# Attention and squared-ReLU layers on one core: softmax sums inverted in pairs, a copy ranked with the other evacuations, and late tiles marked urgent when their pass ends

## The chip, the cores and the metric

The kernel runs on one core of a Trainium2 chip. A core has five engines with instruction streams of their own: TensorE (PE in the profile; its weight loads are PEld), VectorE (DVE), ScalarE (ACT), GpSimd (POOL) and SyncE (SP), which here issues all transfers. The metric is the device time of one execution in microseconds (us); the lower the better.

## What is computed

Two transformer layers over 2048 rows of width 448, with shared weights. Each layer normalizes the rows, does full multi-head attention with 16 heads of 28 columns, adds the result to the rows, normalizes again, and adds a dense layer with a squared ReLU:

```python
x = x + _A_ref(_layernorm(x, axis=-1), A_wqkv, A_wo)
x = x + _B_ref(_layernorm(x, axis=-1), B_w1, B_b1, B_w2, B_b2)
x = x + _A_ref(_layernorm(x, axis=-1), A_wqkv, A_wo)
x = x + _B_ref(_layernorm(x, axis=-1), B_w1, B_b1, B_w2, B_b2)
```

with, inside `_A_ref` and `_B_ref`,

```python
scores = jnp.einsum("bhqd,bhkd->bhqk", q, k) * scale
p = _softmax(scores, axis=-1)
o = jnp.einsum("bhqk,bhkd->bhqd", p, v)
...
r = jnp.where(h > zero, h, zero)
h = r * r
out = jnp.einsum("bsf,fd->bsd", h, w2) + b2
```

The exponentials of the softmax are the largest single piece of work: 2 layers x 16 heads x 2048 x 2048 of them.

## The kernel before

**Tiles and passes.** The 2048 rows are 16 row tiles of 128. Queries go in blocks of two row tiles, 256 rows (`blocks`); the last two blocks of the second layer have one tile each. The 16 heads form four groups of four (`g` from 0 to 3), whose four heads lie in the four quarters of 32 partitions. A pass is a layer, a block of queries, a group of heads and a range of key tiles. A unit is one head with enough key tiles for 512 columns of scores, so that there are 2048 units. Scores have keys on the partitions and queries in the columns.

**Exponentials on two engines.** Three units make up a tile of scores `sc` of 128 x 1536 in PSUM (`s_stream`). ScalarE takes the exponential of it in one instruction and writes `pt` (`e_stream`). From some tiles one unit is set apart for VectorE, which computes its exponential with a polynomial: `a_unit` reads the scores into `v_i` or a free part of `K_sb`, and `a_rest` does five more steps and writes `pd` or another free buffer. ScalarE then takes only the two others, 128 x 1024. Whether a unit is set apart is decided in `apart`, among other things by how full VectorE has been in the last 12 us of the plan.

**Weighted values and sums.** `p_stream` multiplies the exponentials with the values `V_sb` and adds up a pass in a PSUM bank `oT`. The values carry a column of ones behind each head's 28, so that partition 28 of each quarter of `oT` holds the sums of the exponentials. When a pass is done, the bank is evacuated to `oT_sb` (lines L988, L990).

**Division by the sums.** `norm_stream` inverts the sums of one group and multiplies. For most blocks the sums are first spread over all partitions by a transfer (`spread`, L1026, `dn<-oT_sb`), inverted there by a short reciprocal on VectorE (L1032), stored to DRAM (L1038, `scr<-dn`), and read back to all partitions of their head (L1045, `rec<-scr`); then VectorE multiplies `oT_sb` by `rec` into `oTn` (L1049). That is three transfers, one reciprocal and one multiply for each group. The last block of each layer instead uses a matmul with `sel` and a long reciprocal (L1011, L1017).

**The rest of a block.** Once a block's four groups are done, `chain` does the output projection (`wo`), adds to the rows (L1060), normalizes, does the two dense matmuls with `relu` and `square` (L1104, L1108), and in the first layer normalizes again and projects the second layer's queries, keys and values (`qkv`). `layernorm` turns the normalized rows `xn` on TensorE (L478), and an evacuation copies the turned rows from PSUM to `xnT` (L490).

**What sets the order.** All of it is one program whose order is fixed when it is built. A `Planner` keeps a clock for each engine and a list of streams with priorities, lower numbers first. It picks again and again the instruction that can start soonest by estimated durations and latencies, and the priority decides between equals. Buffers are counted by `Res`. Scores have priority 0, exponentials 1, `p_stream` 2, evacuations of matmuls `EV` = 3.5, blocks' chains 4 and up, and VectorE's steps on a unit set apart 6 (`V_PRIO`), then 3.6 (`V_LATE`) when they have waited 5 us of the plan, then 1.8 (`V_LAST`) when ScalarE is `V_AGE` = 5 tiles past the unit's. When TensorE's load in the plan is low, `s_stream` repeats the score matmuls of a tile, and `heat` inserts matmuls that nothing reads (L1158). A repeated `x18` instead of `x6` in the timeline shows such a tile. So a change of a priority or a buffer moves many instructions of all engines.

Of the kernel before, what the change touches and what calls it, by code (L numbers as in the profile page):

```python
# [11 lines left out]
DT = mybir.dt  # L12
AF = mybir.ActivationFunctionType
ALU = mybir.AluOpType
P = 128
# [39 lines left out]
V_PRIO = 6.0  # L55
V_LATE = 3.6
V_LAST = 1.8
V_AGE = 5
OWN3 = 0
FIRST = 90  # L60
V_FIRST = 9.2
# [7 lines left out]
BUSY = 0.95  # L69
SPAN = 12.0  # L70
NPT = 11
NOS = 4
AEND = 8
HOT = 0.9
MORE = 3
# [140 lines left out]
def kernel(  # L216
# [221 lines left out]
    def layernorm(t0, nt, deps_of, early=False, mv=None, place=None):  # L438


        if mv is None:
            mv = moments()
            for j in range(nt):
                yield stats(mv, t0, j, deps_of(j))
        ln = {}
        single = early and t0 == 0 and TILES
        rss = []
        for a, b in [(0, 1), (1, 2)] if single else [(0, nt)]:
            def rsqrt(e, a=a, b=b):
                rstd = sp.tile([P, 4], DT.float32, name="rstd")  # L450
                for j in range(a, b):
                    ln[j] = rstd[:, j:j + 1]
                ve = sp.tile([P, 4], DT.float32, name="ve")
                nc.gpsimd.tensor_tensor(out=ve[:, a:b], in0=mv[0][:, a:b, 1], in1=eps_t[:, a:b], op=ALU.add)  # L454
                nc.gpsimd.tensor_tensor(out=rstd[:, a:b], in0=ve[:, a:b], in1=mhalf[:, a:b], op=ALU.pow)
            rs = Op("POOL", 0.95, rsqrt, deps=[mv[1][b - 1]], sets=[("rs", t0 + a)] if early else ())
            rss += [rs] * (b - a)
            pl.spawn(EV, iter([rs]))
        box = {}

        def take(e):
# [6 lines left out]
        evs = []  # L468

        def turn(p0, own, xs):  # L470
            box = {}

            def tr(e, xs=xs):
                tp = bank(t, "tp").bitcast(DT.bfloat16).rearrange("p (c q) -> p c q", c=NDC)
                box["t"] = tp
                for k, (xn, _) in enumerate(xs):
                    for dc in range(NDC):
                        nc.tensor.transpose(out=tp[:, dc, k * P:(k + 1) * P],  # L478
                                            in_=xn[:, dc * P:(dc + 1) * P], identity=ident[:, :])
            t = Op("PE", 0.07 * NDC * len(xs), tr, deps=[x[1] for x in xs],  # L480
                   acq=pools_now(early) if early else spare(1))
            yield t

            def ev(e, p0=p0, w=len(xs) * P):
                tp = box["t"]
                dst = xnT[:, :, p0 * P:p0 * P + w]
                if e == "ACT":
                    nc.scalar.copy(out=dst, in_=tp[:, :, 0:w])
                else:
                    nc.vector.tensor_copy(out=dst, in_=tp[:, :, 0:w])  # L490
            o = Op("DVE", 0.12 + 0.3 * len(xs), ev, deps=[t], rel=t, sets=[("xT", t0 + p0)] if early else ())
            ends.append(o)
            evs.extend([o, Op("DVE", 0.0, None, deps=[t], rel=own)])

        wide = 1 if single else 2
        for p0 in range(0, nt, wide):
            js = range(p0, min(p0 + wide, nt))
            own = Op("DVE", 0.0, None, acq=R_xn)
            yield own
            xs = []  # L500
            for j in js:
                xn = xns[2 * (own.turn % 2) + j % 2]

                def norm(e, j=j, xn=xn):
                    nc.vector.tensor_scalar(out=xn[:, 0:D], in0=x_sb[:, t0 + j, :],  # L505
                                            scalar1=mv[0][:, j, 0:1], scalar2=ln[j],
                                            op0=ALU.subtract, op1=ALU.mult)
# [12 lines left out]

    def mm_tile(subs, evac, ev_dur, deps, any_engine=False, sets=(), early=False, post=(), acq=None):
# [343 lines left out]
    def a_unit(gi, x, src, unit, l):  # L865
# [14 lines left out]
                apart_from(gi, t)  # L880
        c = Op("DVE", 0.69, take, deps=[("s", gi)], acq=sets_of(unit), rel=x)
        yield c
        pl.spawn(lambda now: V_LAST if e_now[1] - gi >= V_AGE else V_LATE if now > c.end + V_WAIT else V_PRIO if gi > FIRST else V_FIRST, a_rest(gi, c, box, unit, (b0, b1, b2, b3)))

    def a_rest(gi, c, box, unit, bs):
        b0, b1, b2, b3 = bs
# [24 lines left out]
        yield o  # L911

    norm_done = {}
    oTn_of = {}

    def p_stream():


        for pi, (l, qb, g, kbs, first, last) in enumerate(passes):
# [58 lines left out]
                yield o  # L978
            res = {}
            def ev(e, box=box, first=first, last=last, g=g, res=res, n=n, l=l, qb=qb):  # L980
                src = box["t"][:, 0:n]
# [9 lines left out]
            oe = Op("DVE", 0.15 + n / 930, ev, deps=[o], rel=box["o"], acq=R_os if last else None)  # L991
            yield oe
            if last:
                pl.spawn(3, norm_stream(l, qb, g, res, oe))

    def norm_stream(l, qb, g, res, oe):


        t0, nt = blocks[l][qb]
        n = nt * P  # L1000
        box = {}
        tail = qb == len(blocks[l]) - 1
# [5 lines left out]
        if tail:  # L1008
            def den(e):
                box["t"] = bank(d, "den")  # L1010
                nc.tensor.matmul(box["t"][:, 0:n], lhsT=sel[:, :], rhs=res["t"][:, 0:n], start=True, stop=True)  # L1011
            d = Op("PE", 0.1 + n * 4 / 2400, den, deps=[oe], acq=pools_now())
            yield d

            def rcp(e):
                box["r"] = rp.tile([P, QR], DT.float32, name="rec")
                nc.vector.reciprocal(out=box["r"][:, 0:n], in_=box["t"][:, 0:n])  # L1017
            r = Op("DVE", n * 0.0066, rcp, deps=[d], rel=d, acq=R_rec)
            own = r
            yield r  # L1020
        else:
            w = n // DHP

            def spread(e):
                box["d"] = sp.tile([P, QR // DHP], DT.float32, name="dn")
                nc.sync.dma_start(out=box["d"][:, 0:w],  # L1026
                                  in_=res["t"][DH::DHP, 0:n])
            d1 = Op("DMA", 0.5, spread, deps=[oe], lat=1.0)
            yield d1

            def rcp(e):
                nc.vector.reciprocal(out=box["d"][:, 0:w], in_=box["d"][:, 0:w])  # L1032
            r1 = Op("DVE", 0.25, rcp, deps=[d1])
            yield r1

            def away(e):
                box["s"] = dp.tile([P, w], DT.float32, name=f"scr{w}")
                nc.sync.dma_start(out=box["s"][:, :], in_=box["d"][:, 0:w])  # L1038
            d2 = Op("DMA", 0.4, away, deps=[r1], lat=-0.5)
            yield d2  # L1040

            def back(e):
                box["r"] = rp.tile([P, QR], DT.float32, name="rec")
                src = box["s"][:, :].rearrange("(h a) j -> h (a j)", h=G)
                nc.sync.dma_start(out=box["r"][:, 0:n], in_=src.unsqueeze(1).to_broadcast([G, DHP, n]))  # L1045
            r = own = Op("DMA", 0.5, back, deps=[d2], acq=R_rec, lat=2.7)
            yield r
        def mul(e):
            nc.vector.tensor_tensor(out=oTn_of[l, qb][0][:, g, 0:n], in0=res["t"][:, 0:n],  # L1049
                                    in1=box["r"][:, 0:n], op=ALU.mult)  # L1050
        m = Op("DVE", 0.13 + n / 930, mul, deps=[r, oTn_of[l, qb][1]], rel=oe)
        yield m
        yield Op("DVE", 0.0, None, deps=[m], rel=own)
        norm_done.setdefault((l, qb), []).append(m)
        if len(norm_done[l, qb]) == G:
            pl.spawn(LASTP if (l, qb) == (1, len(blocks[1]) - 1) else NLP + 0.1 * (qb - len(blocks[1])) if l == 1 and qb >= len(blocks[1]) - NL else 4 + 0.1 * qb, chain(l, qb))

    def add_to_x(tb, lo=0, hi=D):
        def f(e, t):
# [147 lines left out]
```

The softmax here doesn't subtract the row's maximum and nothing guards it: scores larger than these inputs give would overflow.

## Time and profile before

| | before |
|---|---|
| time, median of 3 runs | 903.86 us (903.23 to 904.43) |
| span of the profiled execution | 901.8 us |
| busy: TensorE, VectorE, ScalarE | 833.8, 798.2, 874.6 us |
| exponentials on ScalarE | 556 of 128x1536, 127 of 128x1024 |
| transfers `dn<-oT_sb`, `scr<-dn`, `rec<-scr` | 60 each |
| bytes moved by transfers | 18.44 MB |

How to read it: the busy time of an engine is the time in which it executes something, and two instructions that overlap are counted once. A mean duration is that of one instruction by itself, so that a count times a mean can exceed the busy time. An engine that is busy all the time need not be the one that sets the end; the tables by stage and the lists of waits tell that. A wait is put down to the instruction whose end released it.

### The profile page before, as it was taken

The page shows a single profiled execution, that of the slowest core. Times are in us where ns is not written, and L with a number is a line of the kernel's source. Part 1 is how long each engine was busy: PE and PEld are TensorE (multiplying, and loading weights), DVE is VectorE, ACT ScalarE, POOL GpSimd, SP SyncE. Part 2 cuts the span into 40 slices and gives each one's busy share as a digit, 9 for nine tenths or more (in the row PEclk, how much of TensorE's full clock was granted, in tenths as well). Part 3 has the DMA queues.
Part 4 walks back from the last instruction along what each step waited for, and adds up shares of the span by engine and source line. Part 5 has one row for each costly group of instructions (what it writes and reads, how often), then busy time and mean ns, then how long its engine had stood idle before and what let it go on. Part 6 is the DMA issues. An engine that isn't in the chain of part 4 may idle for free.

```text
span 901.8 us, 29143 instructions
## 1 busy us (share of the span) xinstructions
PE 833.8 (92%) x12828; PEld 459.2 (51%) x12828; DVE 798.2 (89%) x1628; ACT 874.6 (97%) x702; POOL 41.8 (5%) x100
## 2 busy tenths in 40 slices
PE   8999999999999989989999999888989999999898
PEld 4555544454545445445455455444454544546566
DVE  7999899899999899987889999989999998998664
ACT  6999999999999999999999999999999999999992
POOL 4100000000000010000000000000000000000000
PEclk9999999999999999989999999999999999999999
DMA  7200100000000000000000000011000000000100
GB/s 224 75 2 3 27 27 8 15 14 9 14 14 9 14 15 8 14 8 8 2 1 3 2 2 2 6 40 34 19 14 25 14 24 14 20 19 14 29 6 22
DMA packets 32987, 18.44 MB, mean 20 GB/s; under 512 B 17498, under 2 KB 32411, under 8 KB 32860
## 3 DMA queue, kind: packets, MB, share of 16 engines
q1 hardware_dynamic: 32860, 16.58, 6.4%
q8 instruction: 100, 1.64, 0.8%
q14 instruction: 27, 0.22, 0.1%
HBM read 14.26 MB, written 2.07 MB: 18 GB/s over the span
## 4 chain that ended last, share of the span: by engine, by line
ACT 72%; issue 13%; PE 9%; DVE 5%; DMA 1%; SPq 0%; ACTq 0%; DVEq 0%
ACT pt L819 72%; PE mt L539 4%; PE sc L795 2%; PE oT L966 1%; DVE st L432 1%; PE sc L539 1%; DMA V_sb<-in_A_wqkv_dram 1%; DVE K_sb L894 1%; DVE v_h L894 0%; DVE xn L505 0%; DVE x_sb L1060 0%; PE mt L1158 0%; DVE mv L433 0%; DVE v_i L877 0%; DVE K_sb L877 0%
## 5 line engine op out<-in xcount | busy, mean ns | idle before, releaser
L819 ACT ACTIVATE pt<-sc 128x1536 bf16<-128x1536 f32 (+1 forms) x683 | 864.6, 1575 | 4.1 <-PE sc L795 3.9
L795 PE MATMUL sc<-Q_sb,K_sb 32*128 32x256 bf16 (+1 forms) x5840 | 324.5, 266 | 55.4 <-ACT pt L819 48.3
L795 PEld LDWEIGHTS <-K_sb 32*128 32x128 bf16 x5840 | 156.6, 92 | 234.2 <-issue 204.2
L966 PE MATMUL oT<-pt,V_sb 128*32 128x256 bf16 (+1 forms) x4094 | 151.4, 268 | 1.9 <-DVE V_sb L589 1.2
L539 PE MATMUL mt<-xnT,w 128*128 128x256 bf16 (+1 forms) x888 | 117.8, 271 | 0.8
L966 PEld LDWEIGHTS <-V_sb 128*32 128x32 bf16 x4352 | 92.6, 96 | 47.2 <-issue 44.0
L894 DVE SCALAR_TENSOR_TENSOR K_sb<-K_sb 128x512 f32<-128x512 uint16 x165 | 112.8, 684 | 1.5 <-PE mt L539 0.9
L894 DVE SCALAR_TENSOR_TENSOR v_h<-v_h,v_i 128x512 f32<-128x512 f32 x142 | 96.9, 682 | 0.5
L539 PEld LDWEIGHTS <-w 128*128 128x128 bf16 x952 | 78.8, 98 | 35.4 <-issue 26.7
L1104 DVE TENSOR_SCALAR r<-mt 128x512 bf16<-128x512 f32 x105 | 71.8, 684 | 11.5 <-PE mt L539 10.8
L539 PE MATMUL mt<-w,V_sb 128*128 128x448 bf16 (+1 forms) x288 | 69.9, 352 | 0.0
L877 DVE TENSOR_SCALAR v_i<-sc 128x512 int32<-128x512 f32 x71 | 48.6, 685 | 9.9 <-PE sc L795 9.3
L1060 DVE TENSOR_TENSOR x_sb<-x_sb,mt 128x448 bf16<-128x448 bf16 (+1 forms) x64 | 39.0, 609 | 11.6 <-PE mt L539 11.3
L894 DVE SCALAR_TENSOR_TENSOR v_h<-v_i 128x512 f32<-128x512 uint16 x71 | 48.6, 685 | 0.5
L454 POOL TENSOR_TENSOR ve<-mv,eps_t 128x2 f32<-128x2 f32 (+1 forms) x34 | 9.0, 264 | 842.7 <-DVE mv L433 782.5
L1158 PE MATMUL mt<-xn,ident 128*128 128x448 bf16 x134 | 45.5, 359 | 1.0 <-DVE oT_sb L990 0.3
L877 DVE TENSOR_SCALAR K_sb<-sc 128x512 int32<-128x512 f32 x55 | 37.6, 684 | 5.6 <-PE sc L795 5.4
L432 DVE BATCH_NORM_STATS2 st<-x_sb 128x6 f32<-128x448 bf16 x64 | 39.6, 618 | 1.1 <-DMA x_sb<-in_A_x_dram 0.7
L539 PEld LDWEIGHTS <-V_sb 128*128 128x128 bf16 x302 | 24.9, 98 | 24.6 <-issue 10.5
L988 DVE COPY oT_sb<-oT 128x256 f32<-128x256 f32 (+1 forms) x48 | 19.0, 396 | 17.0 <-PE oT L966 16.9
L1108 DVE TENSOR_TENSOR V_sb<-r 128x512 bf16<-128x512 bf16 (+1 forms) x73 | 30.0, 414 | 2.5 <-ACT r L1102 1.9
L539 PE MATMUL mt<-wo,oTn 128*128 128x448 bf16 x128 | 31.6, 355 | 0.1
(101 smaller groups left out, 752.7 us busy)
## 6 DMA issues: line engine op xcount, KB each, us to landing
rec<-scr SPq DMA_DIRECT2D x56, 128.0 KB
x_sb<-in_A_x_dram SPq DMA_DIRECT2D x8, 224.0 KB
out_dram<-x_sb SPq DMA_DIRECT2D x15, 112.0 KB
w<-in_B_w_dram SPq DMA_DIRECT2D x1, 1568.0 KB
w<-in_B_w_dram SPq DMA_DIRECT2D x1, 1344.0 KB
dn<-oT_sb SPq DMA_DIRECT2D x56, 4.0 KB
scr<-dn SPq DMA_DIRECT2D x56, 4.0 KB
V_sb<-in_A_wqkv_dram SPq DMA_DIRECT2D x1, 672.0 KB
```

The source lines that it names most:

```text
L432: nc.vector.bn_stats(out=st[:, :], in_=x_sb[:, t0 + j, :])
L539: nc.tensor.matmul(box["t"][:, c0:c0 + n], lhsT=lhsT() if callable(lhsT) else lhsT, rhs=rhs, start=a, stop=b)
L795: nc.tensor.matmul(dst[k][:, i * nt * P:(i + 1) * nt * P], lhsT=K_sb[l][rows, g, (kb + i) * P:(kb + i + 1) * P], rhs=Q_sb[rows, g, t0 * P: ...
L819: t = nc.scalar.activation(out=pt[:, 0:n], in_=gbuf[gi]["sc"][:, 0:n], func=AF.Exp, scale=float(np.log(2.0)) * 2.0 ** -FRAC)
L877: t = nc.vector.tensor_scalar(out=box["i"], in0=two(src), scalar1=EXP_BIAS, scalar2=EXP_LOW, op0=ALU.add, op1=ALU.max)
L894: nc.vector.scalar_tensor_tensor(out=box["h"], in0=box["f"] if begin else box["h"], scalar=b, in1=box["f"], op0=ALU.add, op1=ALU.mult)
L966: nc.tensor.matmul(box["t"][DHP * hh:DHP * hh + DHP, 0:n], lhsT=V_sb[l][:, kb + i, 4 * g + hh, :], rhs=p[:, c0:c0 + n], start=begin and kb ...
L988: nc.vector.tensor_copy(out=dst, in_=src)
L1060: nc.vector.tensor_tensor(out=x_sb[:, tb, lo:hi], in0=x_sb[:, tb, lo:hi], in1=t[:, 0:hi - lo], op=ALU.add)
L1104: nc.vector.tensor_scalar(out=r[:, 0:w], in0=t[:, 0:w], scalar1=0.0, scalar2=None, op0=ALU.max)
L1108: nc.vector.tensor_tensor(out=h[:, 0:w // n, :], in0=r, in1=r, op=ALU.mult)
L1158: nc.tensor.matmul(t[:, 0:D], lhsT=ident[:, :], rhs=xns[0][:, 0:D], start=True, stop=True)
```

## The change

It has three parts, which act on one another through the planner.

The first joins two groups of heads in the division. `oT_sb` becomes a tile for two groups, `[P, 2, QR]`, of which there are three instead of four of half the size. `norm_pair` starts when both groups of a pair are evacuated. It issues two spreads, one reciprocal over both, one store, two reads back, and one multiply over both. The last block of each layer keeps its way, group by group (`norm_stream`), with the new tiles. This is for fewer instructions on VectorE and fewer transfers.

The second is in `layernorm`: the copy of the turned rows was an instruction of the block's own stream, with the chain's priority of 4 or more. It now gets a stream of its own with priority `EV`, as other evacuations have. This is to free the PSUM bank sooner and let a block's chain go on.

The third concerns the steps of VectorE on a unit set apart: they get the urgent priority `V_LAST` when ScalarE is 6 tiles past (`V_AGE`), not 5, or when the scores are more than 3 units (`V_PAST`) past the end of the unit's pass. This is so that the end of a pass isn't held up by its last unit.

```diff
-V_AGE = 5
+V_AGE = 6
+V_PAST = 3
...
-NOS = 4
+NOS = 3
...
-            evs.extend([o, Op("DVE", 0.0, None, deps=[t], rel=own)])
+            pl.spawn(EV, iter([o, Op("DVE", 0.0, None, deps=[t], rel=own)]))
...
-        yield from evs
...
-        pl.spawn(lambda now: V_LAST if e_now[1] - gi >= V_AGE else V_LATE if now > c.end + V_WAIT else V_PRIO if gi > FIRST else V_FIRST, a_rest(gi, c, box, unit, (b0, b1, b2, b3)))
+        pl.spawn(lambda now: V_LAST if e_now[1] - gi >= V_AGE or at[0] > ends_at[unit[0]] + V_PAST else V_LATE if now > c.end + V_WAIT else V_PRIO if gi > FIRST else V_FIRST, a_rest(gi, c, box, unit, (b0, b1, b2, b3)))
...
-                    dst = res["t"] = osp.tile([P, QR], DT.float32, name="oT_sb")
+                    dst = res["t"] = pair["t"][:, g % 2, :]
...
+                if qb == len(blocks[l]) - 1:
+                    pl.spawn(3, norm_stream(l, qb, g, res, oe, pair))
+                elif len(pair["ev"]) == 2:
+                    pl.spawn(3, norm_pair(l, qb, g - g % 2, pair))
...
+    def norm_pair(l, qb, g, pair):
...
+            for i in range(2):
+                nc.sync.dma_start(out=box["d"][:, i, 0:w], in_=both[DH::DHP, i, :])
+        d1 = Op("DMA", 0.9, spread, deps=pair["ev"], lat=1.0)
...
+            nc.vector.reciprocal(out=box["d"][:, :, 0:w], in_=box["d"][:, :, 0:w])
+        r1 = Op("DVE", 0.33, rcp, deps=[d1])
...
+            nc.sync.dma_start(out=box["s"].rearrange("(i p j) -> p i j", i=2, p=P), in_=box["d"][:, :, 0:w])
...
+            for i in range(2):
+                src = box["s"][i * P * w:(i + 1) * P * w].rearrange("(h k) -> h k", h=G)
+                nc.sync.dma_start(out=box["r"][:, i, 0:n], in_=src.unsqueeze(1).to_broadcast([G, DHP, n]))
+        r = Op("DMA", 0.9, back, deps=[d2], acq=R_rec, lat=2.7)
...
+            nc.vector.tensor_tensor(out=oTn_of[l, qb][0][:, g:g + 2, 0:n], in0=both,
+                                    in1=box["r"][:, :, 0:n], op=ALU.mult)
```

More of the change, by code (lines that the diff above doesn't have):

```diff
@@ L467, in layernorm @@
         todo = []
-        evs = []
         def turn(p0, own, xs):
@@ L913 @@
     norm_done = {}
+    pairs = {}
     oTn_of = {}
@@ L980, in ev @@
             def ev(e, box=box, first=first, last=last, g=g, res=res, n=n, l=l, qb=qb):
+                pair = pairs.get((l, qb, g // 2))
                 src = box["t"][:, 0:n]
                 if last:
-                    dst = res["t"] = osp.tile([P, QR], DT.float32, name="oT_sb")
+                    dst = res["t"] = pair["t"][:, g % 2, :]
                     dst = dst[:, 0:n]
@@ L990, in ev, with both, norm_start @@
                     nc.vector.tensor_tensor(out=dst, in0=src, in1=part(l, qb, g), op=ALU.add)
-            oe = Op("DVE", 0.15 + n / 930, ev, deps=[o], rel=box["o"], acq=R_os if last else None)
+            if last and (l, qb, g // 2) not in pairs:
+                def both(e, l=l, qb=qb, g=g):
+                    pairs[l, qb, g // 2]["t"] = osp.tile([P, 2, QR], DT.float32, name="oT_sb")
+                pairs[l, qb, g // 2] = {"own": Op("DVE", 0.0, both, acq=R_os), "ev": [], "res": []}
+                yield pairs[l, qb, g // 2]["own"]
+            pair = pairs[l, qb, g // 2] if last else None
+            oe = Op("DVE", 0.15 + n / 930, ev, deps=[o], rel=box["o"])
             yield oe
             if last:
[L994 to L1002, printed above, removed]
+                pair["ev"].append(oe)
+                pair["res"].append((g, res))
+                if qb == len(blocks[l]) - 1:
+                    pl.spawn(3, norm_stream(l, qb, g, res, oe, pair))
+                elif len(pair["ev"]) == 2:
+                    pl.spawn(3, norm_pair(l, qb, g - g % 2, pair))
+    def norm_start(l, qb):
         if (l, qb) not in oTn_of:
@@ L1007, in norm_stream @@
             yield oTn_of[l, qb][1]
[L1008 to L1047, printed above, removed]
@@ new lines, in norm_end, with norm_stream, den, rcp @@
+    def norm_end(l, qb, m, gs):
+        norm_done.setdefault((l, qb), []).extend([m] * gs)
+        if len(norm_done[l, qb]) == G:
+            pl.spawn(LASTP if (l, qb) == (1, len(blocks[1]) - 1) else NLP + 0.1 * (qb - len(blocks[1])) if l == 1 and qb >= len(blocks[1]) - NL else 4 + 0.1 * qb, chain(l, qb))
+    def norm_stream(l, qb, g, res, oe, pair):
+        t0, nt = blocks[l][qb]
+        n = nt * P
+        box = {}
+        yield from norm_start(l, qb)
+        def den(e):
+            box["t"] = bank(d, "den")
+            nc.tensor.matmul(box["t"][:, 0:n], lhsT=sel[:, :], rhs=res["t"][:, 0:n], start=True, stop=True)
+        d = Op("PE", 0.1 + n * 4 / 2400, den, deps=[oe], acq=pools_now())
+        yield d
+        def rcp(e):
+            box["r"] = rp.tile([P, 2, QR], DT.float32, name="rec")[:, 0, :]
+            nc.vector.reciprocal(out=box["r"][:, 0:n], in_=box["t"][:, 0:n])
+        r = Op("DVE", n * 0.0066, rcp, deps=[d], rel=d, acq=R_rec)
+        yield r
@@ L1050, in mul @@
                                     in1=box["r"][:, 0:n], op=ALU.mult)
-        m = Op("DVE", 0.13 + n / 930, mul, deps=[r, oTn_of[l, qb][1]], rel=oe)
+        m = Op("DVE", 0.13 + n / 930, mul, deps=[r, oTn_of[l, qb][1]])
         yield m
[L1053 to L1056, printed above, removed]
+        yield Op("DVE", 0.0, None, deps=[m], rel=r)
@@ new lines, in norm_stream, with spread, rcp, away @@
+        pair.setdefault("mul", []).append(m)
+        if len(pair["mul"]) == 2:
+            yield Op("DVE", 0.0, None, deps=[m], rel=pair["own"])
+        norm_end(l, qb, m, 1)
+    def norm_pair(l, qb, g, pair):
+        n = blocks[l][qb][1] * P
+        box = {}
+        yield from norm_start(l, qb)
+        w = n // DHP
+        both = pair["t"][:, :, 0:n]
+        def spread(e):
+            box["d"] = sp.tile([P, 2, QR // DHP], DT.float32, name="dn")
+            for i in range(2):
+                nc.sync.dma_start(out=box["d"][:, i, 0:w], in_=both[DH::DHP, i, :])
+        d1 = Op("DMA", 0.9, spread, deps=pair["ev"], lat=1.0)
+        yield d1
+        def rcp(e):
+            nc.vector.reciprocal(out=box["d"][:, :, 0:w], in_=box["d"][:, :, 0:w])
+        r1 = Op("DVE", 0.33, rcp, deps=[d1])
+        yield r1
+        def away(e):
+            box["s"] = dp.tile([P, 2 * w], DT.float32, name=f"scr{w}")[:, :].rearrange("p k -> (p k)")
+            nc.sync.dma_start(out=box["s"].rearrange("(i p j) -> p i j", i=2, p=P), in_=box["d"][:, :, 0:w])
+        d2 = Op("DMA", 0.4, away, deps=[r1], lat=-0.5)
+        yield d2
+        def back(e):
+            box["r"] = rp.tile([P, 2, QR], DT.float32, name="rec")
+            for i in range(2):
+                src = box["s"][i * P * w:(i + 1) * P * w].rearrange("(h k) -> h k", h=G)
+                nc.sync.dma_start(out=box["r"][:, i, 0:n], in_=src.unsqueeze(1).to_broadcast([G, DHP, n]))
+        r = Op("DMA", 0.9, back, deps=[d2], acq=R_rec, lat=2.7)
+        yield r
+        def mul(e):
+            nc.vector.tensor_tensor(out=oTn_of[l, qb][0][:, g:g + 2, 0:n], in0=both,
+                                    in1=box["r"][:, :, 0:n], op=ALU.mult)
+        m = Op("DVE", 0.13 + 2 * n / 930, mul, deps=[r, oTn_of[l, qb][1]], rel=pair["own"])
+        yield m
+        yield Op("DVE", 0.0, None, deps=[m], rel=r)
+        norm_end(l, qb, m, 2)
```

## The prediction

> **What bounds the kernel now.** I read four views in this order: the page's totals, a table of busy time by stage, ScalarE's list of waits, and the groups by form.
>
> ```profile
> PE 833.8 (92%) x12828; PEld 459.2 (51%) x12828; DVE 798.2 (89%) x1628; ACT 874.6 (97%) x702; POOL 41.8 (5%) x100
> ```
>
> Three engines look full; the share alone doesn't say which one sets the end. The table by stage does (stretch; length; busy time and instructions of PE, PEld, DVE, ACT, POOL; granted clock; DMA):
>
> ```profile
> 0.00:11.16 11.16, 9.21 (x58) 5.19 (x59) 7.93 (x33) 4.88 (x9) 4.75 (x14) 1.00 0.87 270
> 11.16:30.00 18.84, 17.05 (x217) 9.36 (x215) 15.64 (x37) 17.20 (x15) 7.22 (x15) 1.00 0.62 195
> 30.00:300.00 270.00, 254.52 (x3817) 139.51 (x3812) 250.52 (x505) 270.00 (x215) 10.15 (x26) 1.00 0.05 12
> 385.00:410.00 25.00, 22.58 (x325) 11.76 (x324) 18.23 (x36) 22.52 (x18) 1.06 (x4) 0.86 0.04 12
> 410.00:881.62 471.62, 437.44 (x7059) 240.47 (x7059) 417.83 (x840) 471.62 (x374) 13.99 (x32) 1.00 0.05 14
> 881.62:901.80 20.18, 16.39 (x199) 12.20 (x196) 9.19 (x22) 3.97 (x8) 0.75 (x2) 1.00 0.06 19
> ```
>
> ScalarE is busy for 270.00 of 270.00 us and again for 471.62 of 471.62. From its first exponential at 11.16 us to the end of its last at 881.62 us it is the limit; VectorE (417.83 of 471.62) and TensorE have slack there. Its losses in between are few:
>
> ```profile
> ACT pt L819 <- PE sc L795: 3.9, 7, 1.3
> ```
>
> Of these 3.9 us, 1.1 belong to the opening (0.91 and 0.19), 0.43 to 303.98 us, and 2.4 to the change of layer, where ScalarE's timeline shows them:
>
> ```profile
> 386.17 13.60 ACT L819 ACTIVATE pt<-sc 128x1536 bf16<-128x1536 f32 x11 [0.52 <-PE sc L795]
> 400.05 2.97 ACT L819 ACTIVATE pt<-sc 128x1536 bf16<-128x1536 f32 x2 [0.28 <-PE sc L795]
> 404.30 1.45 ACT L819 ACTIVATE pt<-sc 128x1536 bf16<-128x1536 f32 x1 [1.28 <-PE sc L795]
> ```
>
> The last two, with one of 0.34 us at 406.09, make 1.9 us and fall where TensorE's granted clock fell:
>
> ```profile
> 395.00:400.00 5.00, 3.51 (x64) 2.14 (x62) 5.00 (x10) 4.77 (x4) 0.00 (x0) 0.78 0.00 0
> 400.00:405.00 5.00, 5.00 (x41) 2.16 (x36) 2.68 (x6) 3.60 (x3) 0.00 (x0) 0.54 0.02 4
> ```
>
> First TensorE has little to do (3.51 us) while VectorE is full, then it works at 0.54 of its clock and ScalarE waits. So the time is: 11.16 us of start, the sum of the exponentials, about 4 us of waits, and a tail of 20.18 us.
>
> The pieces of the sum, and the VectorE groups that the change touches:
>
> ```profile
> L819 ACT ACTIVATE pt<-sc 128x1536 bf16<-128x1536 f32 x556 | 776.8, 1652 | 4.1 <-PE sc L795 3.9
> L819 ACT ACTIVATE pt<-sc 128x1024 bf16<-128x1024 f32 x127 | 146.0, 1235 | 0.0
> L1049 DVE TENSOR_TENSOR oTn<-oT_sb,rec 128x256 bf16<-128x256 f32 x60 | 24.8, 415 | 0.2 <-DMA rec<-scr 0.2
> L1032 DVE RECIPROCAL dn<-dn 128x8 f32<-128x8 f32 x56 | 10.7, 192 | 0.6 <-DMA dn<-oT_sb 0.6
> ```
>
> Exponentials overlap their neighbours, so a mean duration is not what one costs. The step of an exponential of 128x1024 is 0.417 us shorter than one of 128x1536 by mean (1652 less 1235 ns). By starts in the chain of waits, 52.11 to 53.44 us is 1.33 for the wide one; 53.44 to 55.68 is one wide and one narrow, so 0.91. I take a difference of 0.427 us: with it, 374 exponentials (304 wide, 70 narrow) in 471.62 us give 1.341 and 0.914, near those steps.
>
> [...] a 128x512 f32 step lasts 684 ns, a 128x256 f32 multiply 415. But neighbours overlap, and from start to start they are 0.60 us (300.81 to 301.41) and 0.33 us (299.54 to 299.87), so merging two spares only 0.06 us. [...] Here the sync queue waited for the 4 KB store of inverted sums 49 times for 66.1 us, 1.35 us each; measured is what I use.
>
> **The change part by part.** I compared the two programs' instruction orders, which are fixed when they are built.
>
> *Pairs.* Reciprocals go from 60 to 30. One steps about 0.10 us (387.91 to 388.01); of double size I take 0.11, as 8 more elements are worth 8 ns at the multiply's rate: 60 x 0.10 - 30 x 0.11 = 2.7 us saved on VectorE. Multiplies: 28 wide ones replace 56, 28 x 0.06 = 1.7 us. Together 4.4 us, none on ScalarE's path, so worth nothing by themselves. Transfers go from 180 to 150, on a queue that isn't on the path. The added wait: a pair's reciprocal waits for two spreads, issued 0.54 us each, and its multiply for two returns, 0.52 us each, so each becomes ready about half a microsecond later. Queued behind it is all of VectorE's work, and TensorE waits for that. But VectorE's order moves too: by the rows' durations, the work between the last evacuation and the reciprocal has a median of 4.0 us after and 3.8 before, between reciprocal and multiply 7.2 after and 6.7 before. Before, these two waits cost 0.6 and 0.2 us in all. I take 0; the worst, 0.3 us at 30 pairs, is 9 us of VectorE, less than the 53.8 us it has idle after 410 us alone (471.62 less 417.83).
>
> *Rank of the copy of transposed rows, age, and end of pass.* These move work. The one direct effect on the path is a count: the new order has 552 wide and 131 narrow exponentials where the old has 556 and 127. In tiles of 512 columns, 556 x 3 + 127 x 2 = 1922, now 552 x 3 + 131 x 2 = 1918: VectorE computes 130 of the 2048 tiles, not 126. ScalarE's sum falls by 4 x 0.427 = 1.71 us. VectorE pays for a tile five steps at 0.60 us and one at 0.34 (302.61 to 302.95), 3.34 us: 13.4 us for four. Net of the 4.4 it does 9.0 us more, 807 us or 89%: still under the limit, and hidden beside ScalarE.
>
> *Where it moves.* In the old order the query projections of layer 1's fifth, sixth and seventh pair of row tiles end at exponentials 315, 353 and 403 (counted from 0), in the new one at 300, 342 and 387. The eighth pair's move from 437 to 433. So the blocks' chains around the change of layer run 11 to 16 exponentials earlier, 14 to 20 us at the mean step of 1.26 us (471.62 / 374). The fifth pair's key and value projections, which stand at exponentials 305 to 310 in the old order and so at 401 to 408 us, inside the stretch with the low clock, are past by then.
>
> *TensorE.* 258 more score matmuls (repeats that keep it busy) and 22 fewer fillers. Eighteen take 0.83 us where six take 0.39, so 37 ns each: 258 x 0.037 = 9.5 us, less 22 fillers at 0.34 us (45.5 us of busy time for 134 in their group), 7.5 us. It fills slack. Summing its work between exponentials at full rate, the old order has 44 stretches of six exponentials with under 0.6 of TensorE's time filled, the new one 26; the thinnest of the old, 0.51, is just before the clock fell, and the new has none below 0.53.
>
> *Head and tail.* The first exponentials and everything on TensorE after the last scores are the same list in both: 11.16 and 20.18 us stay.
>
> **The sum.** 903.86 - 1.71 for the exponentials = 902.15. The half-clock stretch most likely goes, -1.9. Against it I charge 0.5 us for new waits of the kind of 0.43 and 0.52 us, which VectorE's extra 9 us makes likelier. That gives 900.75.
>
> **The rivals.** *Only the count.* The clock falls somewhere else instead, or the waits keep their sum: 902.15. For it: the new order still has stretches at 0.53 to 0.55. Against it: they are fewer. *All inner waits go*: 903.86 - 1.71 - 2.85 (0.43, 0.52 and 1.9) = 899.3. For it: two long stretches already have none. *Cancelled*: VectorE's 9 us turns into waits of ScalarE that eat the 1.71 and the 1.9 stays: about 903.9. *Slower*: the longer pair transfers hold VectorE, TensorE starves twice, and each time the clock falls at 1.9 us on top of the old one: 902.15 + 3.8 = 905.95. For it: VectorE is full for ten microseconds at a time (390 to 400); against it: DMA waits cost 0.8 us in the whole trace, and the new distances have grown with the transfers.
>
> **How the numbers follow.** Forecast case 0.47, only the count 0.24, all waits gone 0.10, cancelled 0.11, slower 0.08. Within 0.2% is 902.05 to 905.67. Faster takes nearly all of the first (0.43), all of the third (0.10) and under half of the second (0.11): 0.64. Slower than 905.67 is 0.08, as the last case has a longer side; the rest, 0.28, is the same. The range runs from the case without waits, 899.3, to the cancelled one, 903.9; some 0.1 lies above it and some 0.08 below.
>
> **What would show it.** Right: 552 and 131 exponentials with unchanged steps, so their stretch is about 1.7 us shorter; no dip of the granted clock near the change of layer, and ScalarE's wait on the scores near 2.5 us in all; reciprocals and multiplies idle for DMA under 2 us; VectorE near 807 us; a tail of 20.2 us. Wrong: new seconds of low clock, waits of ScalarE of more than 4 us, or VectorE idle for DMA by several microseconds with the scores waiting behind it.

## The result and the profile after

| | before | after |
|---|---|---|
| time, median | 903.65 us (4 runs) | 900.11 us (4 runs, 898.66 to 900.23) |
| ratio to before, 95% interval | | 0.9956 (0.9939 to 0.9973) |
| span of the profiled execution | 901.8 us | 898.1 us |
| start to the first exponential | 11.16 | 11.44 |
| first exponential to the end of the last | 870.46 | 866.39 |
| tail behind the last exponential | 20.18 | 20.27 |

The kernel became 3.5 us faster, 0.44%. In the profiled executions all of it lies between the first and the last exponential (4.07 us less); the start and the tail are 0.4 us longer together. The table by stage of the kernel after, cut there (stretch; length; busy time and instructions of PE, PEld, DVE, ACT, POOL; granted clock; DMA):

```profile
11.44:877.83 866.39, 809.27 (x12810) 445.51 (x12809) 788.98 (x1538) 863.65 (x686) 36.33 (x85) 1.00 0.06 17
877.83:898.10 20.27, 16.39 (x199) 12.20 (x196) 9.19 (x22) 3.97 (x7) 0.75 (x2) 0.99 0.06 19
```

ScalarE is busy for 863.65 of 866.39 us, so it is still the limit. The tail has the same busy times and counts of instructions on TensorE and VectorE as before, to the last digit. The groups by form of the kernel after, for the exponentials, the multiplies and the reciprocals:

```profile
L818 ACT ACTIVATE pt<-sc 128x1536 bf16<-128x1536 f32 x552 | 772.7, 1649 | 2.2 <-PE sc L794 2.1
L818 ACT ACTIVATE pt<-sc 128x1024 bf16<-128x1024 f32 x131 | 150.7, 1226 | 0.0
L1088 DVE TENSOR_TENSOR oTn<-oT_sb,rec 128x512 bf16<-128x512 f32 x28 | 19.1, 683 | 1.8 <-DMA rec<-scr 1.8
L1069 DVE RECIPROCAL dn<-dn 128x16 f32<-128x16 f32 x28 | 6.8, 243 | 0.0
```

Four wide exponentials became narrow, as the order said, and the multiplies wait for their transfers for 1.8 us in all, where it was 0.2. The page's lists have 806.2 us of VectorE and 872.5 of ScalarE. ScalarE's list of waits after:

```profile
ACT pt L818 <- PE sc L794: 2.1, 4, 0.9
```

Before, it was 3.9 us in seven waits. Two of the four are the opening's, as before (0.91 and 0.19 us). The other two are new and stand in ScalarE's timeline after:

```profile
521.39 1.45 ACT L818 ACTIVATE pt<-sc 128x1536 bf16<-128x1536 f32 x1 [0.61 <-PE sc L794]
523.23 10.00 ACT L818 ACTIVATE pt<-sc 128x1536 bf16<-128x1536 f32 x8 [0.38 <-PE sc L794]
```

The table by stage around them says why; the third figure from the end is the granted clock:

```profile
515.00:517.50 2.50, 1.48 (x36) 0.76 (x26) 2.34 (x6) 2.50 (x3) 0.00 (x0) 1.00 0.00 0
517.50:520.00 2.50, 1.98 (x29) 1.46 (x25) 2.50 (x5) 2.50 (x3) 0.00 (x0) 0.80 0.03 7
520.00:522.50 2.50, 2.50 (x32) 1.04 (x33) 1.31 (x4) 1.89 (x2) 0.00 (x0) 0.51 0.00 0
```

So the dip of the clock at the change of layer is gone, and a shorter one has come: the trace's record of the granted clock has half speed from 519.0 to 522.4 us, for 3.41 us, after a stretch in which TensorE was busy for 1.48 of 2.50 us. Before, it had half speed from 397.8 to 404.6 us, for 6.83 us, twice as long, and after a stretch as thin (1.54 of 2.50 us):

```profile
395.00:397.50 2.50, 1.54 (x36) 0.97 (x31) 2.50 (x6) 2.50 (x3) 0.00 (x0) 1.00 0.00 0
397.50:400.00 2.50, 1.96 (x28) 1.17 (x31) 2.50 (x5) 2.27 (x3) 0.00 (x0) 0.56 0.00 0
```

Of the four runs of the kernel after, three had a mean clock of 0.998 and took 900.03 to 900.23 us; the fourth kept 1.000 and took 898.66.

### The profile page after: what moved, and what is told of

Read it like the earlier page. It is cut to its first block, busy times and chain, and to the rows that moved or that the text cites. A ratio compares the mean times of both kernels' runs of the same rounds, so it can differ in the third digit from the quotient of the medians.

```text
span 898.1 us, 29569 instructions
## 1 busy us (share of the span) xinstructions
PE 835.5 (93%) x13064; PEld 463.5 (52%) x13064; DVE 806.2 (90%) x1592; ACT 872.5 (97%) x702; POOL 41.8 (5%) x100
## 4 chain that ended last, share of the span: by engine, by line
ACT 71%; issue 12%; PE 12%; DVE 4%; DMA 1%; POOL 0%; SPq 0%; DVEq 0%; ACTq 0%
ACT pt L818 71%; PE mt L538 4%; PE sc L794 3%; PE oT L966 2%; DVE st L433 1%; PE mt L325 1%; PE sc L538 1%; DMA rec<-scr 1%; DVE xn L505 0%; DVE x_sb L1097 0%; DMA scr<-dn 0%; DVE K_sb L893 0%; DVE mv L434 0%; DVE xnT L490 0%; PE mt L1195 0%
## 5 line engine op out<-in xcount | busy, mean ns | idle before, releaser
L818 ACT ACTIVATE pt<-sc 128x1536 bf16<-128x1536 f32 (+1 forms) x683 | 862.5, 1568 | 2.2 <-PE sc L794 2.1
L794 PE MATMUL sc<-Q_sb,K_sb 32*128 32x256 bf16 (+1 forms) x6098 | 332.5, 265 | 53.1 <-ACT pt L818 48.0
L794 PEld LDWEIGHTS <-K_sb 32*128 32x128 bf16 x6098 | 162.8, 92 | 230.5 <-issue 199.6
L893 DVE SCALAR_TENSOR_TENSOR K_sb<-K_sb 128x512 f32<-128x512 uint16 x168 | 114.9, 684 | 0.9 <-PE mt L538 0.2
L893 DVE SCALAR_TENSOR_TENSOR v_h<-v_h,v_i 128x512 f32<-128x512 f32 x148 | 101.1, 683 | 0.3
L876 DVE TENSOR_SCALAR v_i<-sc 128x512 int32<-128x512 f32 x74 | 50.7, 685 | 10.1 <-PE sc L794 9.9
L893 DVE SCALAR_TENSOR_TENSOR v_h<-v_i 128x512 f32<-128x512 uint16 x74 | 50.7, 685 | 0.7
L1195 PE MATMUL mt<-xn,ident 128*128 128x448 bf16 x112 | 38.6, 357 | 0.2
L505 DVE TENSOR_SCALAR xn<-x_sb,mv,rstd 128x448 bf16<-128x448 bf16 x64 | 24.9, 410 | 8.6 <-POOL rstd L456 8.3
```

What stands on the lines that cost most here:

```text
L794: nc.tensor.matmul(dst[k][:, i * nt * P:(i + 1) * nt * P], lhsT=K_sb[l][rows, g, (kb + i) * P:(kb + i + 1) * P], rhs=Q_sb[rows, g, t0 * P: ...
L818: t = nc.scalar.activation(out=pt[:, 0:n], in_=gbuf[gi]["sc"][:, 0:n], func=AF.Exp, scale=float(np.log(2.0)) * 2.0 ** -FRAC)
L876: t = nc.vector.tensor_scalar(out=box["i"], in0=two(src), scalar1=EXP_BIAS, scalar2=EXP_LOW, op0=ALU.add, op1=ALU.max)
L893: nc.vector.scalar_tensor_tensor(out=box["h"], in0=box["f"] if begin else box["h"], scalar=b, in1=box["f"], op0=ALU.add, op1=ALU.mult)
L1195: nc.tensor.matmul(t[:, 0:D], lhsT=ident[:, :], rhs=xns[0][:, 0:D], start=True, stop=True)
```

## The experiments

After the result the theory was: no part of the change has a price of its own, except through the order it makes; the time is the start, the exponentials' sum (0.427 us for each unit that ScalarE doesn't have to do), ScalarE's waits, about half of them behind a dip of TensorE's clock (1.9 of 3.9 us before, 0.99 of 2.1 after), and the tail. The rivals: the pairs bring the gain by freeing VectorE, or the parts add up. The first eight kernels tell these apart. Each measured ratio is to the kernel before, run beside it; only the parts of an edit that bear on the argument are shown.

**Each part alone.** The rank alone, on the kernel before:

```diff
-            evs.extend([o, Op("DVE", 0.0, None, deps=[t], rel=own)])
+            pl.spawn(EV, iter([o, Op("DVE", 0.0, None, deps=[t], rel=own)]))
...
-        yield from evs
```

> The kernel before with the copy of turned rows ranked with the other evacuations, and nothing else of the change. Its order has 552 wide and 131 narrow exponentials, so VectorE takes 130 units, as in the whole change. Theory of the count: ScalarE's sum falls by 4 x 0.427 = 1.7 us, so 902.0 or less, and lower by up to 1.9 where the granted clock doesn't fall at the change of layer. Rival, that the pairs of head groups bring the gain by freeing VectorE: nothing is freed here and VectorE has 13.4 us more to do, so 903.7 or above.

Measured: 906.63 us, ratio 1.0032 (1.002 to 1.0045). Slower, though VectorE takes 130 units as in the whole change, so the time of 902.0 or less was missed by over 4 us. The count came true (552 and 131), and the rival's reason is not it either: with 13 us more for VectorE the exponentials' stretch is no longer than before (869.71 and 870.46 us). What spoils it is at the end, told below.

The pairs alone, on the kernel before (`norm_pair` and the tiles of two groups, as in the change):

```diff
-NOS = 4
+NOS = 3
...
+                elif len(pair["ev"]) == 2:
+                    pl.spawn(3, norm_pair(l, qb, g - g % 2, pair))
```

> The kernel before with the pairs of head groups alone. Its order has 554 wide and 129 narrow exponentials, 128 units on VectorE. Theory of the count: 903.65 - 2 x 0.427 = 902.8, give or take a stretch of low clock of up to 1.9 us. Rival, that pairs bring the gain: near 900.1, the time of the whole change.

Measured: 906.07 us, ratio 1.0023 (1.0015 to 1.0031). Slower, and 3.3 us above what the count gave, so the pairs by themselves bring nothing.

The urgency alone, on the kernel before (of the long line, the part that changes):

```diff
-V_AGE = 5
+V_AGE = 6
+V_PAST = 3
...
-V_LAST if e_now[1] - gi >= V_AGE else V_LATE
+V_LAST if e_now[1] - gi >= V_AGE or at[0] > ends_at[unit[0]] + V_PAST else V_LATE
```

> The kernel before with the urgency of late tiles alone. Its order has 557 wide and 126 narrow exponentials, 125 units on VectorE. Theory of the count: 903.65 + 0.43 = 904.1, give or take a stretch of low clock of up to 1.9 us. Rival, that the end of a pass was held up by its last unit and the urgency frees it: ScalarE's waits of 4.1 us shrink, 902 or below.

Measured: 902.94 us, ratio 0.9996 (0.9988 to 1.0004). No difference that the interval shows. In its profile ScalarE's waits did shrink, to 2.0 us, as the rival said, but the tail is 2.7 us longer.

**Each part left out of the whole.** The edits are those above, reversed, on the kernel after. Without the rank:

```diff
-            pl.spawn(EV, iter([o, Op("DVE", 0.0, None, deps=[t], rel=own)]))
+            evs.extend([o, Op("DVE", 0.0, None, deps=[t], rel=own)])
...
+        yield from evs
```

> The whole change without the new rank of the copy of turned rows. Its order has 556 wide and 127 narrow exponentials, as the kernel before: 126 units on VectorE, but the pairs still spare it about 4.4 us. Theory of the count: 903.65, less what the waits at the change of layer lose, so 901.7 to 903.7. Rival, that VectorE's own time bounds the kernel in stretches: the 4.4 us spared come off, 899 to 900.

Measured: 902.8 us, ratio 0.9993 (0.9986 to 1.0). Within what the count expects; the pairs' spared time does not come off.

Without the urgency:

```diff
-V_AGE = 6
-V_PAST = 3
+V_AGE = 5
...
-V_LAST if e_now[1] - gi >= V_AGE or at[0] > ends_at[unit[0]] + V_PAST else V_LATE
+V_LAST if e_now[1] - gi >= V_AGE else V_LATE
```

> The whole change without the urgency of late tiles: pairs and rank. Its order has 554 wide and 129 narrow exponentials, 128 units on VectorE, two fewer than the whole change. Theory now, after the single parts: no part has a gain of its own, each moves the order, and the time is the head, the count, the waits and the tail of that order. By the count alone it stands 0.85 us above the whole change, 901.0; a tail of 22 to 24 us in place of 20.3, as rank alone and pairs alone have, would put it at 903 to 905. Rival, that parts add up: rank (+3.0) and pairs (+2.5) together give 909.

Measured: 904.79 us, ratio 1.0022 (1.0014 to 1.003), as expected with a long tail.

Without the pairs:

```diff
-NOS = 3
+NOS = 4
...
-                    pl.spawn(3, norm_pair(l, qb, g - g % 2, pair))
+                pl.spawn(3, norm_stream(l, qb, g, res, oe))
```

> The whole change without the pairs: rank and urgency. Its order has 557 wide and 126 narrow exponentials, 125 units on VectorE, five fewer than the whole change. By the count alone it stands 5 x 0.427 = 2.1 us above it, 902.2, more where its tail is longer than 20.3 us. Rival, that parts add up: rank (+3.0) and urgency (-0.6) give 906.0.

Measured: 904.95 us, ratio 1.0018 (1.001 to 1.0027): the count's 902.2 and the 2.7 us by which its tail is longer make 904.9.

The parts don't add up: rank and pairs, which lose 3.0 and 2.5 us alone by the medians, lose 1.5 together (2.9, 2.1 and 2.0 by the ratios) and gain with the urgency. The eight corners, with the pieces of each one's profiled execution in us, the matmuls behind its last exponential, and where and for how long the clock was halved before that program's last matmuls:

| kernel | units on VectorE | start | exponentials' stretch | of it, waits on scores | tail | matmuls in the tail | clock halved |
|---|---|---|---|---|---|---|---|
| before | 126 | 11.16 | 870.46 | 3.9 | 20.18 | 199 | 6.8 at 398 |
| rank | 130 | 11.06 | 869.71 | 4.1 | 24.53 | 191 | 3.4 at 18, 6.8 at 885 |
| pairs | 128 | 11.46 | 869.64 | 4.2 | 21.90 | 201 | 3.4 at 144 |
| urgency | 125 | 11.10 | 867.96 | 2.0 | 22.84 | 209 | 3.4 at 679 |
| pairs, urgency | 126 | 11.48 | 867.87 | 1.6 | 20.25 | 199 | no |
| pairs, rank | 128 | 11.79 | 866.79 | 1.6 | 24.72 | 191 | 3.4 at 846, 6.8 at 884 |
| rank, urgency | 125 | 11.70 | 869.06 | 1.2 | 22.94 | 209 | 3.4 at 19 |
| all (after) | 130 | 11.44 | 866.39 | 2.1 | 20.27 | 199 | 3.4 at 519 |

Each row is one execution. With the waits taken off and 0.427 us put on for each unit above 126 (taken off for the one below), the stretches are 865.5 to 866.6 us, but 867.3 and 867.4 in the two rows whose clock was halved at 18 or 19 us. There ScalarE also waits for TensorE before its copies of keys and values, 2.3 and 2.8 us against 0.7 before, which the column of waits leaves out. So the theory of pieces holds to about 0.5 us either way where the opening is undisturbed. Some 1.2 us of the stretch in these two rows is likely the execution's and not the order's, as the same opening has this dip in one execution and not in another: the kernel with 126 units, below, has it at 18 us, and the whole change does not.

The whole change has the shortest stretch in these executions and, what no one of its parts aims at, kept the short tail. The rank's loss is such a tail. Its table by stage, behind the last exponential at 880.77 us:

```profile
880.00:885.00 5.00, 3.21 (x44) 1.58 (x43) 3.21 (x7) 0.77 (x1) 0.53 (x2) 1.00 0.07 23
885.00:890.00 5.00, 3.19 (x29) 3.03 (x30) 2.44 (x6) 0.60 (x1) 0.98 (x3) 0.52 0.01 3
890.00:895.00 5.00, 5.00 (x75) 5.00 (x73) 2.03 (x5) 1.97 (x4) 0.00 (x0) 0.80 0.00 0
```

and that of the whole change, behind 877.83 us:

```profile
880.00:885.00 5.00, 4.69 (x66) 3.80 (x64) 4.36 (x10) 1.39 (x3) 0.75 (x2) 1.00 0.07 23
885.00:890.00 5.00, 4.93 (x73) 4.17 (x71) 2.86 (x8) 2.57 (x5) 0.00 (x0) 1.00 0.01 3
```

With the rank alone the last block's chain finds TensorE with little else to do (3.21 of 5.00 us; it stands still three times for VectorE, 3.6 us in all), the clock is halved from 885.2 to 892.0 us, and the first of the dense matmuls that end the program run at that clock. In the whole change other dense matmuls fill the same place (4.69 and 4.93 of 5.00 us), and the clock stays at 1.00. A tail can also be long at full clock: with the urgency alone, with rank and urgency, and with the pairs alone it is 1.7 to 2.8 us longer than before, with other lists of matmuls and a wait of 1.3 to 1.9 us for VectorE in them.

**What a unit on VectorE is worth.** In the kernel after, none is set apart once there are 106; the scores, the values and the result's computation stay complete:

```diff
+        if len(taken) >= 106:
+            return None
```

> The whole change, but once 106 units have been set apart for VectorE none is any more, so that ScalarE gets the last 24 of the 130. Theory of the count: 24 x 0.427 = 10.2 us more on ScalarE, 910.3, while VectorE has some 80 us less to do. Rival, that VectorE bounds the kernel too and units set apart cost about what they save: 900 to 903.

Measured: 907.07 us, ratio 1.0054 (1.0041 to 1.0067). The table by stage of this kernel:

```profile
11.32:887.62 876.30, 816.27 (x12990) 452.16 (x12990) 713.86 (x1396) 873.79 (x686) 35.55 (x85) 1.00 0.06 17
887.62:905.00 17.38, 13.48 (x177) 10.55 (x174) 7.84 (x20) 3.97 (x8) 0.75 (x2) 0.99 0.05 14
```

The exponentials' stretch is 9.91 us longer for 24 units, with 0.3 us less of waits (1.8 us), so 0.43 us for each: the step of 0.427 holds. VectorE has 75.1 us less to do in it, 3.13 a unit, and that brings nothing there. But the tail is 2.9 us shorter, which the expectation of 910.3 had missed: only 177 matmuls are left behind the last exponential, where the whole change has 199.

**What VectorE's spared time is worth.** The kernel after with the pair's work on VectorE written as two and two instructions, at the same places of the same order:

```diff
+            for i in range(2):
+                nc.vector.reciprocal(out=box["d"][:, i, 0:w], in_=box["d"][:, i, 0:w])
...
+            for i in range(2):
+                nc.vector.tensor_tensor(out=oTn_of[l, qb][0][:, g + i, 0:n], in0=both[:, i, :],
+                                        in1=box["r"][:, i, 0:n], op=ALU.mult)
```

> The whole change with the same order of everything, but the reciprocal and the multiply of a pair are written as two instructions each, which gives VectorE back the 4.4 us that pairs spare it. Theory: hidden beside ScalarE, 899.9 to 900.5. Rival, that VectorE's saved time is what the pairs bring: 902 to 904.5.

Measured: 899.64 us (898.81 to 899.67), ratio 0.996 (0.9948 to 0.9972), no slower than the whole change. Its table by stage:

```profile
11.49:876.49 865.00, 807.73 (x12810) 444.98 (x12810) 791.37 (x1598) 863.28 (x686) 35.69 (x85) 1.00 0.06 17
```

VectorE has 60 instructions and 2.4 us more than in the whole change (791.37 against 788.98), and the stretch isn't longer; this execution had no dip of the clock and 1.0 us less of waits, and is 1.4 us shorter. So the time that pairs spare on VectorE is hidden, and it was 2.4 us, not 4.4. It has the same order as the whole change, and the same thin place at 515 us, where its clock did not fall:

```profile
515.00:520.00 5.00, 3.46 (x64) 2.12 (x55) 4.84 (x11) 5.00 (x5) 0.00 (x0) 1.00 0.01 3
```

So with the same work of TensorE, 3.46 of 5.00 us from 515 us on, the clock fell at 519.0 us in the whole change's execution and stayed at 1.00 in this one: the thin stretch does not make it fall each time.

**What the thin stretches do.** In the kernel before, more repeats of the score matmuls are written out in the thin stretch ahead of the dip, without telling the planner, so that the order stays:

```diff
+                again = max(again, {299: 1, 300: 1, 301: 3, 303: 2}.get(gi, 0))
```

> The kernel before with the order kept, and 6 more score matmuls at exponentials 299, 300 and 301 and 12 more at 303, in the thin stretch before the clock fell at the change of layer. Theory: the dip at 397 to 405 us goes, and the waits of 1.9 us with it: 901.7, and more runs at a mean clock of 0.998 and above. Rival, that the crowd of projections at 400 to 408 us makes the waits by itself: 903.6.

Measured: 901.86 us, ratio 0.9992 (0.9985 to 0.9998). Thirteen of its 21 runs kept a mean clock of 1.000, none of the 25 runs of the kernel before beside it. The table by stage at the place of the old dip:

```profile
395.00:400.00 5.00, 3.88 (x80) 2.74 (x80) 5.00 (x11) 4.96 (x5) 0.00 (x0) 1.00 0.00 0
400.00:405.00 5.00, 4.85 (x78) 2.85 (x78) 4.50 (x10) 4.97 (x4) 0.00 (x0) 1.00 0.03 4
```

TensorE does 0.4 us more in the thin part, the clock stays at 1.00, and ScalarE is busy for 4.97 us where it was 3.60, with the crowd of projections still at the same place in the order. The three waits of 1.9 us are gone. So they came from the clock and not from the crowd.

The same in the kernel after, ahead of 518 us:

```diff
+                again = max(again, {395: 1, 396: 3, 398: 2}.get(gi, 0))
```

> The whole change with the order kept, and 6 more score matmuls in front of exponential 395, 6 more at 396 and 12 more at 398, which write the scores again where TensorE waited for ScalarE just before its clock fell. Theory: the thin stretch is what lets the clock fall, so the dip at 515 to 522 us goes and with it 1.3 us, 898.6 to 898.9, as in the one run without a dip (898.66). Rival, that the dip comes from elsewhere or the repeats hold up the scores: 900.1 or above.

Measured: 899.59 us (898.79 to 901.52), ratio 0.9965 (0.9952 to 0.9977). Three of five runs kept 1.000 and took 899.13 us on average; two had 0.998 and took 900.8. The profiled one has no dip at 518 us. By the ratio to the kernel before it is no better than the whole change, and the runs are few: this doesn't show a gain, and the time lies between the expectation and its rival.

**Leaving the last units to ScalarE.** The shorter tail with 106 units suggested to leave only the last few to ScalarE:

```diff
+        if len(taken) >= 126:
+            return None
```

> The whole change, but once 126 units have been set apart for VectorE none is any more, so the last four of the 130 stay with ScalarE. Up to there the order is that of the whole change. ScalarE gets 4 x 0.427 = 1.7 us more; behind the last scores the order leaves TensorE 13.5 us of matmuls where the whole change leaves 17.0, so the tail falls from 20.3 us towards the 17.4 of the kernel with 106. Theory of head, exponentials and tail: 900.1 + 1.7 - 2.9 = 898.9. Rival, that the count alone sets the time: 901.8.

Measured: 898.83 us (897.93 to 899.89), ratio 0.9954 (0.9942 to 0.9966) to the kernel before, whose median beside it was 902.74. The tail was 17.05 us. At a mean clock of 0.998 its three runs took 898.24 us on average, the whole change's three 900.15, and the kernel before 902.49 beside these three and 902.76 at another time. So it surely beats the kernel before. By the ratio of all runs it only equals the whole change (0.9954 and 0.9956), as half of its six runs had a mean clock of 0.996, and the profiled one of these two dips, at 18 and at 520 us; that it is the better order is likely, by some 1.6 us at equal clock, and not shown, since the two did not run side by side.

```diff
+        if len(taken) >= 128:
+            return None
```

> As the kernel with 126, but with the last two of the 130 units left to ScalarE. ScalarE gets 0.85 us more; TensorE has 14.6 us of matmuls behind the last scores instead of 17.0, so the tail should be some 18 us. Theory of head, exponentials and tail: 900.1 + 0.85 - 2.3 = 898.7. Rival, that the count alone sets the time: 901.0.

Measured: 904.67 us, ratio 1.0019 (1.001 to 1.0028). A miss, by 6 us. The tables by stage in the tail, of the kernel with 128:

```profile
880.00:885.00 5.00, 1.48 (x12) 0.78 (x11) 3.68 (x9) 0.00 (x0) 1.35 (x4) 0.86 0.00 0
885.00:890.00 5.00, 5.00 (x50) 5.00 (x49) 1.58 (x4) 1.19 (x2) 0.15 (x1) 0.50 0.02 3
```

and of the kernel with 126:

```profile
880.00:885.00 5.00, 5.00 (x81) 4.07 (x77) 2.87 (x7) 2.71 (x5) 0.00 (x0) 1.00 0.02 3
885.00:890.00 5.00, 4.21 (x45) 2.88 (x44) 2.39 (x7) 0.45 (x2) 0.75 (x2) 1.00 0.07 23
```

With 128 the tail is 25.07 us: TensorE has less left to do, as expected (191 matmuls), but it stands still for 3.5 of the 5 us from 880 us on, and has half its clock from 883.6 to 890.5 us. A tail is not the sum of its matmuls.

## Why the prediction was right, and where it was not

- *The count.* Right: 552 and 131. The group of the exponentials lost 2.1 us of busy time (864.6 to 862.5), where the step was put at 1.71. The rest is likely the waits themselves: an exponential that starts after a wait stands for 1.45 us in the timelines instead of its step of 1.34, and there are three waits fewer, 0.33 us. The 0.427 for a unit was measured at 0.43 with 24 units.
- *The dip at the change of layer goes.* It did, and the waits fell by 1.8 us (3.9 to 2.1), where the forecast had 1.9 less 0.5. The reason given was half wrong. That the chains run earlier and so crowd 385 to 410 us less isn't needed: with the old crowd in place and the clock kept up, the three waits of 1.9 us are gone. What the run shows to count is the thin stretch ahead of it: with TensorE busy for 3.88 of 5.00 us there instead of 3.51, the clock stayed at 1.00. The size of 1.9 us is that of an execution with a mean clock of 0.996. With the thin stretch filled and the clock at 1.000 the kernel before took 901.65 us, 2.2 us less than beside it at 0.996 (903.83) and 1.0 less than at 0.998 (902.62), so for a run with a shorter dip the term was about twice what it came to.
- *No stretch thinner than 0.53.* This step failed. It summed TensorE's work over six exponentials, some 8 us, and found the new order thicker. The clock fell nonetheless, at exponentials 398 to 400. Over four exponentials, some 5 us, the same sum gives 0.43 at 395 as the thinnest of the new order and 0.44 at 300 as that of the old one, and these are the two places where the clock fell. Taken over again from the start times in the traces, the sum is thinnest within one exponential of the same two places; with the pairs alone and with the urgency alone it is thinnest just ahead of their dips, too. So a window of four exponentials would have shown it. That a thin stretch lets the clock fall was at that time the author's estimate, from one place of the trace before (3.51 of 5.00 us of work, then a granted clock of 0.54), and how long a stretch has to be for it no run shows. The rival that the clock falls somewhere else thus came true in its event, though not in its size: the new dip is half as long as the old one and cost ScalarE 0.99 us of waits. A new stretch of low clock was also named as a sign of being wrong.
- *0.5 us for new waits.* The waits of 0.43 and 0.52 us went too, and the new dip's 0.61 and 0.38 took their place. So the sum was near for a reason other than the one given.
- *The pairs are hidden.* Right, and shown by writing them as single instructions. Their saving was put at 4.4 us and measured at 2.4, which changes nothing. The multiplies' waits for transfers stayed under the 2 us allowed, and VectorE came out at 806.2 us (807 forecast).
- *Start and tail.* The tail is the same list and took 20.27 us. The start was 0.28 us longer; over all profiled executions it lies between 11.06 and 12.13 us, and kernels with the same beginning differ by as much (11.10 and 11.44 us for the version with 126 units and the whole change), so this is scatter.

The median of 900.11 us is 0.64 below the forecast. At an equal mean clock of 0.998 the whole change is 2.6 us below the kernel before (900.15 against 902.76, means of 3 and of 22 runs, not taken side by side); the remaining 0.9 us is likely how often and for how long the clock falls. That the prediction came out so near leans on luck: rank or pairs alone, whose orders could have been counted in the same way, took 906 us, mostly because of a tail that the sum held constant. Here the last part of TensorE's list was compared, and it was the same. That comparison carried the forecast, more than the count: every kernel here with the list of 199 matmuls has a tail of 20.1 to 20.3 us, and those with another list have 17.0 to 25.1.

What stays open: why the planner's order has a short tail with all three parts and with pairs and urgency, and not with the others. Nothing here says that it is more than chance.

## What to carry to other kernels

In a program whose order a planner writes, read a change as a new order: count what the limiting engine must do, compare the list behind its last instruction, and look for thin stretches of TensorE over windows of a few microseconds: here the clock fell after 1.54 and 1.48 of 2.50 us of work. A part that loses alone can be part of a gain, so test the corners before naming a cause. And time that an engine saves beside the limit was worth nothing here (2.4 us of VectorE by the pairs), while holes of about 3.5 us on TensorE ahead of a dense end went with tails 4 to 5 us longer (24.53 us with the rank alone and 25.07 with 128 units, against 20.18 before).

## What the runs showed of the hardware

The same program takes different times, and here the longer ones mostly went with a lower mean granted clock of TensorE. In the trace's record of the clock, its fall before the program's last matmuls lasted 6.83 us in the kernel before and 3.41 us in the kernel after, at half speed. In the tables by stage of the other profiled executions, each such fall comes to about 3.4 or 6.8 us at half speed. One of 3.41 us takes 1.7 us, or 0.002, off the mean clock of 900 us, and the profiled executions agree: the mean clock is 0.996 before, with 6.83 us, 0.998 after, with 3.41 us, and 1.000 without the rank, with no fall. So how long a run was at half speed can be estimated from its mean clock.

The kernel without the rank ran 21 times: 901.68 us on average at a mean clock of 1.000 (7 runs), 902.86 at 0.998 (7), 903.86 at 0.996 (6), and 902.60 once at 0.997. The pairs alone took 903.74, 905.01, 906.41 and 907.81 us at 1.000, 0.998, 0.996 and 0.994. So in these two kernels a mean clock lower by 0.002, by that estimate a fall of 3.41 us, went with 1.0 to 1.4 us more, though ScalarE is the limit.

TensorE was not idle ahead of these falls. The clock fell after stretches in which it was busy for 1.54 of 2.50 us (the kernel before, 395.0 to 397.5 us) and 1.48 of 2.50 us (after, 515.0 to 517.5 us). How little work is too little isn't measured. Nor is why the clock falls in one execution of an order and not in the next: three of the four runs of the kernel after had a mean clock of 0.998 and one kept 1.000.
